# One loop per engine for two attention branches, with branch A's sums folded behind the loops

## The chip, the cores and the metric

The kernel runs on one core of a Trainium2 chip. The metric is the device time of one execution in microseconds. The engines are named as the profile names them: PE multiplies matrices (PEld is its loading of weights), DVE works on vectors, ACT on scalars and activations, POOL is GpSimd, and SP issues the loads.

## What is computed

Two attention branches, A and B, decode one token for two batch entries from a cache of 4096 tokens, 32 heads of 128 elements, all in float32. A gate mixes them. Cut to what matters:

```python
def branch(x, k_cache, v_cache, wq, wo):      # x: 2 x 1 x 512, caches: 2 x 32 x 4096 x 128
    q = heads_of(x @ wq)                      # wq: 512 x 4096
    p = softmax(q @ k_cache^T * 128 ** -0.5)  # over the 4096 tokens
    return rows_of(p @ v_cache) @ wo          # wo: 4096 x 512

g = sigmoid((A_x * gate_w).sum(-1))
out = g * branch(A_x, A_...) + (1 - g) * branch(A_x, B_...)
```

The work is hardly more than reading four caches of 134 MB each once.

## The kernel before

**Tiling.** A unit of work is one branch, one group `g` of four heads (`NG = 8` groups) and one batch entry `b`. There are `NU = 32` units, all of A's before all of B's. A unit's K block and V block are 8 MB each: 128 partitions, on each of them 128 tokens of 128 elements, 32 partitions to a head. K blocks alternate between the two tiles `kt`, V blocks share one tile `vt`. `wq` of both branches comes through `kt` before the first units, and `wo` of both after the last ones (A's into the tile that holds even units, B's into the other).

**The loads.** SP issues all large loads in one written order (lines 516 to 526): `wq` of A, the first K block, `wq` of B, then K and V by turns, `wo` of A, the last V block in three parts, `wo` of B in six parts. In front of a K load it waits until DVE has read the tile's last block (`k_free`), in front of a V load until PE has (`v_free`).

**A unit.** DVE multiplies the K block by the query (line 391) and sums it to scores (394). It takes the maxima over a head (399 to 401) and spreads the next query (404, 405). ACT makes the exponentials (365) into `padded` and their sums into a column of `lp`. PE multiplies them by V in 64 matmuls (`products`, line 369) and adds up both batch entries of a group in the PSUM tile `vp`. When a group is through, ACT (452) and DVE (415) add `vp` into `vs[:, g]`.

**The end of a branch.** `sum_of` (lines 467 to 470) makes the denominators from `lp`, times the gate. `gather` (473) collects `vs[:, g]` in the PSUM tile `heads`, two matmul records for each of the eight groups. `deal_out` scales them on ACT (478), puts them in the order that `wo` wants with 16 matmul records against the table `deal` (482), and copies the result to `on[n]` (485). `project_out` (497) multiplies by `wo`. The last rows of B's `wo` are done in four strips (512), and the rest, `most`, is folded into them (609, 612) with `fold`, which is made from an identity that POOL writes (589, 590, 592).

**Loops.** The engines run free of each other and meet at semaphores. PE, DVE and ACT have hardware loops of their own. Each branch has its own loops over its first seven groups: DVE and ACT leave theirs for the last group of A. In that straight part DVE does A's `sum_of`, PE A's eight gathers and `deal` matmuls, and ACT A's copies (`branch_sums`, and the argument `between` of `dve_first` and `act_first`); then the loops of B begin. PE's first loop takes 16 units, its second 15. A's projection stands behind PE's second loop, and B's last unit and end follow it. The table `deal` is built by DVE in the first microseconds (313 to 318), from the identity that lies in `vt` then.

All of this is written out by hand inside one unscheduled part (`tile_critical`, line 179).

Of the kernel before, what the change touches and what calls it, by code (L numbers as in the profile page):

```python
# [7 lines left out]
F32 = mybir.dt.float32  # L8
# [5 lines left out]
B = 2  # L14
# [6 lines left out]
NG = H // G  # L21
NS = SK // PH
# [119 lines left out]
def tile_gated_decode(ctx: ExitStack, tc: tile.TileContext, ins: dict, out: bass.AP):  # L142
# [9 lines left out]
    gate = {n: small.tile([P, 1], F32, name="gate" + n) for n in "AB"}  # L152
# [15 lines left out]
    nil = small.tile([P, 1], F32, name="nil")  # L168
# [10 lines left out]
    with tc.tile_critical():  # L179
# [10 lines left out]
        r_vs = [R() for _ in range(NG)]  # L190
# [122 lines left out]
        put("dve", lambda x: x.memset(deal, 0.0), [], [r_deal])  # L313
        for b in range(B):
            for k in range(DQ):
                piece = R()
                piece.writers = r_deal.writers[:1]
                vput("dve", lambda x: x.tensor_copy(deal[:, b, k, :, :, k], ident.rearrange(
                    "p (h g b) -> p b g h", h=G, b=B)[:, b, :NG]), [r_ident], [piece])
        r_deal.writers = piece.writers  # L320
# [4 lines left out]
        def project(n):  # L325
            i_k = place["wq", n]
            if n == "A":
                room, mark = Scratch(vt, 8 * P + D), lambda p: r_vt.readers.append(p)
            else:
                room, mark = Scratch(kt[i_k]), lambda p: None  # L330
            halves = kt[i_k].rearrange("p r d -> p (r d)").rearrange(
                "p (c i g h d) -> p c i h g d", c=KC, i=NG // STRIPS, h=G, d=DH)
            for i, t in enumerate(qa):
                put("dve", lambda x: x.memset(t, 0.0), [], [r_qa[i]])
            for c in range(KC):
                arrived("pe", ("wq", n), *((c * len(parts["wq", n]) // KC,)))
                for i, t in enumerate(qa):
                    for h in range(G):
                        put("pe", lambda x: x.matmul(t[h * QT:h * QT + B], cols[:, c], halves[:, c, i, h],  # L339
                                                     start=c == 0, stop=c == KC - 1), [r_cols, *r_kt[i_k]], [r_qa[i]])  # L340
# [10 lines left out]
            mark(put("dve", lambda x: x.tensor_copy(qcol[n], wide.rearrange("p (g k b) -> p g k b", g=NG, b=QT)[:, :, :, :B]),  # L351
                     [r_wide], [r_qcol[n]]))
            for r in r_kt[i_k]:
                r.readers += r_wide.readers

        def spread_queries(u):
            n, g, b = units[u]
            put("dve", lambda x: x.tensor_copy(qsel, qcol[n][:, g:g + 1, :, b:b + 1]), [r_qcol[n]], [r_qsel])
            put("dve", lambda x: x.transpose(q, qsel[:, 0].to_broadcast([P, DH // QT, QT])), [r_qsel], [r_q])
# [43 lines left out]
        def next_queries(n, g, b):  # L403
            at = D_.do(lambda x: x.tensor_copy(qsel, qcol[n][:, g, :, b:b + 1]))  # L404
            return D_.do(lambda x: x.transpose(q, qsel[:, 0].to_broadcast([P, DH // QT, QT])), at)  # L405

        def dve_second(nxt):
            take("dve", k_landed[1], 16)
            maxima_of(1, whole_scores(1, 0))
            return next_queries(*nxt, 0) if nxt else 0  # L410
# [7 lines left out]
        def dve_first(g, nxt, at, between=None):  # L418
# [4 lines left out]
            if between:  # L423
                between()
            maxima_of(0, at)
            next_queries(*nxt, 1)
# [27 lines left out]
        def act_first(g, col, between=None):  # L454
# [5 lines left out]
            if between:  # L460
                between()
# [3 lines left out]

        def sum_of(n):
            put("dve", lambda x: x.transpose(across, lp), [r_lp], [r_across])
            put("dve", lambda x: x.tensor_reduce(rs, across, axis=AX.X, op=ALU.add), [r_across], [r_rs])
            put("dve", lambda x: x.reciprocal(rs, rs), [], [r_rs])
            put("dve", lambda x: x.tensor_tensor(rs, rs, gate[n], op=ALU.mult), [r_gate[n]], [r_rs])  # L470

        def gather(g):
            put("pe", lambda x: x.matmul(heads, pick[:, (NG - g) * B:][:, :P], vs[:, g], start=g == 0, stop=g == NG - 1),
                [r_pick, r_vs[g]], [r_heads])

        def deal_out(n):
            t = vs[:, 0]
            put("act", lambda x: x.activation(t, heads, AF.Copy, scale=rs), [r_heads, r_rs], [r_vs[0]])
            dealt = bank[:, :B * OR].rearrange("p (b r) -> p b r", b=B)
            for b in range(B):  # L480
                for k in range(DQ):
                    put("pe", lambda x: x.matmul(dealt[:, b], deal[:, b, k].rearrange("p g h q -> p (g h q)"),
                                                 t[:, k * OR:(k + 1) * OR], start=k == 0, stop=k == DQ - 1),
                        [r_deal, r_vs[0]], [r_bank])
# [59 lines left out]
        def step(e, n, lo, hi, second, first):  # L544
            with nc.Fori(lo, hi, engines=[{"dve": mybir.EngineType.DVE, "act": mybir.EngineType.Activation}[e]]) as i:
                first(i, second(i))

        def dve_pairs(n):
            S.wait("dve", [*r_q.writers, (S.sems["dve"], S.ticks["dve"])])
            with nc.Fori(0, NG - 1, engines=[mybir.EngineType.DVE]) as i:  # L550
                nxt = n, bass.ds(i + 1, 1)
                at = dve_second(nxt)
                dve_first(i, nxt, at)

        def act_pairs():
            with nc.Fori(0, NG - 1, engines=[mybir.EngineType.Activation]) as i:
                act_second(bass.ds(i * B + 1, 1))
                act_first(i, bass.ds(i * B + B, 1))
# [23 lines left out]
        end = Scratch(kt[place["wo", "A"]]).take  # L582
        ident2, fold, onb, kept = end(P), end(QT), end(OR * B), end(D)
        totals = [end(D // OS)[:B].rearrange("b (s e) -> b s e", s=STRIPS // OS) for _ in range(OS)]
        on["B"] = onb.rearrange("p (r b) -> p r b", b=B)
        r_ident2, r_fold, r_kept, r_total = R(), R(), R(), [R(), R()]
        for r in (r_ident2, r_fold, r_kept, r_on["B"], *r_total):
            r.readers = [p for x in r_kt[place["wo", "A"]] for p in x.readers]
        put("pool", lambda x: x.memset(ident2, 0.0), [], [r_ident2])
        put("pool", lambda x: x.affine_select(out=ident2, in_=ident2, compare_op=ALU.not_equal, fill=1.0, base=0,  # L590
                                              pattern=[[-1, P]], channel_multiplier=1), [], [r_ident2])
        put("dve", lambda x: x.tensor_reduce(fold, ident2.rearrange("p (s q) -> p q s", s=STRIPS), axis=AX.X, op=ALU.add),  # L592
            [r_ident2], [r_fold])
        sum_of("B")
        for g in range(NG - 1):
            r_vs[g].writers = r_rs.writers
            gather(g)
        last_products()
        take_out(NG - 1)
        take("dve", taken)  # L600
        for a in range(1, VC):
            put("dve", lambda x: x.scalar_tensor_tensor(  # L602
                vs[:, NG - 1], vp[:, a * DH:(a + 1) * DH], slot[:, a:a + 1], vs[:, NG - 1], op0=ALU.mult, op1=ALU.add),
                [r_vs[NG - 1]] if a > 1 else [], [r_vs[NG - 1]] if a > 1 else [])
            r_vs[NG - 1].writers = [(S.sems["dve"], S.ticks["dve"])]
        gather(NG - 1)
        deal_out("B")
        project_out("B", EARLY)
        put("act", lambda x: x.activation(kept, most, AF.Copy), [r_most], [r_kept])  # L609
# [6 lines left out]
        for i, e in enumerate(("dve", "act")):  # L616
            for j in range(STRIPS // OS):
                k = (i * STRIPS // OS + j) * QT
                src = acc[i][k:k + B, :D // STRIPS]
                put(e, (lambda x: x.activation(totals[i][:, j], src, AF.Copy)) if i else  # L620
                    (lambda x: x.tensor_copy(totals[i][:, j], src)), [r_qa[i]], [r_total[i]])  # L621
            landed.append(S.dma("act" if i else "sp", out.rearrange("b o (i s e) -> (b o) i s e", i=OS, s=STRIPS // OS)[:, i],
                                totals[i], reads=[r_total[i]], slot="x"))
# [23 lines left out]
```

## Time and profile before

| | before |
|---|---|
| median of 3 runs | 1324.59 us (1324.45 to 1324.62) |
| the profiled execution | 1324.58 us |
| its span, first to last instruction | 1322.8 us |
| read from memory | 570.43 MB, 431 GB/s over the span |
| busy: DVE, PE, ACT | 1166.3, 343.3, 101.4 us |
| mean granted clock of PE | 0.627 of full speed |

A row of the timeline begins with its start and its duration in microseconds; then come the engine, the line of the kernel, the operation, what it writes and reads, and how many records the row merges. In brackets stands how long the engine had been idle and what ended that. A "q" behind an engine's name is its instruction queue. A row of the table by stretches gives the stretch, its length, the busy time and number of instructions of PE, PEld, DVE, ACT and POOL, then PE's granted clock, the share of DMA engines that were busy and GB/s. Matmuls overlap, so a merged row's duration is that of the whole stretch and the mean of one record is longer than the spacing.

### The profile page before, as it was taken

The numbers are of one execution on the slowest core, as the hardware profiler recorded it, in microseconds if no ns is written. First come the engines' busy times: TensorE is split into PE (matmuls) and PEld (weight loads), VectorE is DVE, ScalarE is ACT, GpSimd is POOL, SyncE is SP. The second block draws the span as 40 slices with busy tenths as digits, with TensorE's granted clock in tenths as the row PEclk, the third lists the DMA queues.
The fourth block names the chain that finished last, engine by engine and source line by source line (L and its number), as shares of the span: only waits on it lengthen the run. The fifth ranks groups of instructions, "written<-read, shape, count | busy, mean of one in ns | idle before, by whom it ended". The sixth has DMA issues, their size and how long they took to land. (4 is left out here: it accounts for less than half of the span.)

```text
span 1322.8 us, 6257 instructions
## 1 busy us (share of the span) xinstructions
PE 343.3 (26%) x2406; PEld 100.7 (8%) x2406; DVE 1166.3 (88%) x321; ACT 101.4 (8%) x331; POOL 1.2 (0%) x8
## 2 busy tenths in 40 slices
PE   3202222202222221222224022222212222221256
PEld 0000000000000000000002000000000000000012
DVE  2399999999999999999999899999999999999960
ACT  0000000001010000101000010100001010000100
POOL 0000000000000000000000000000000000000000
PEclk9656666556666655666665566666566666656668
DMA  9999999999999999999999999999999999999998
GB/s 412 442 414 442 442 416 442 444 414 444 442 430 428 442 442 416 442 442 416 444 442 419 438 442 434 426 440 440 420 440 440 420 442 442 426 432 442 434 420 357
DMA packets 11109, 570.53 MB, mean 431 GB/s; under 512 B 1239, under 2 KB 1243, under 8 KB 1630
## 3 DMA queue, kind: packets, MB, share of 16 engines
q1 hardware_dynamic: 11092, 570.43, 99.6%
q8 instruction: 4, 0.07, 0.0%
q14 instruction: 3, 0.02, 0.0%
q10 hardware_dynamic: 10, 0.01, 0.0%
HBM read 570.43 MB, written 0.00 MB: 431 GB/s over the span
## 5 line engine op out<-in xcount | busy, mean ns | idle before, releaser
L391 DVE TENSOR_TENSOR kt<-kt,q 128x16384 f32<-128x16384 f32 x31 | 534.0, 17226 | 56.1 <-DVEq L95 56.0
L394 DVE TENSOR_REDUCE sc<-kt 128x128 f32<-128x16384 f32 x31 | 533.8, 17220 | 1.1
L369 PE MATMUL vp<-vt,pr 128*32 128x512 f32 x2048 | 291.8, 733 | 919.3 <-PEq L95 918.5
L369 PEld LDWEIGHTS vp<-vt,pr 128*32 128x32 f32 x2048 | 80.3, 132 | 1129.3 <-issue 1126.9
L365 ACT ACTIVATE pr<-sc,nm 32x128 f32<-32x128 f32 x128 | 50.9, 398 | 160.0 <-ACTq L95 118.2
L431 ACT ACTIVATE pr<-nil 128x512 f32<-128x512 f32 x31 | 19.3, 624 | 426.4 <-ACTq L95 426.4
L452 ACT ACTIVATE vs<-vp,slot 128x128 f32 (+1 forms) x16 | 5.9, 368 | 451.6 <-ACTq L95 451.6
L339 PE MATMUL qa<-kt,cols 128*2 128x512 f32 x128 | 18.7, 741 | 22.9 <-DMA kt<-in_B_wq_dram 15.7
L365 ACT ACTIVATION_READ_ACCUMULATOR pr<-sc,nm (+1 forms) x128 | 23.5, 184 | 0.0
L350 DVE STREAM_TRANSPOSE kt<-kt 128x1024 f32<-128x1024 f32 x1 | 1.2, 1246 | 23.5 <-ACT kt L348 23.5
L415 DVE SCALAR_TENSOR_TENSOR vs<-vp,slot,vs 128x128 f32 (+1 forms) x45 | 15.8, 351 | 6.3 <-DVEq L95 5.3
L534 DVE TENSOR_REDUCE sc<-kt 128x64 f32<-128x8192 f32 x2 | 17.4, 8686 | 0.1
L533 DVE TENSOR_TENSOR kt<-kt,q 128x8192 f32<-128x8192 f32 x2 | 17.4, 8686 | 0.0
L459 ACT ACTIVATE vp<-nil 128x512 f32<-128x512 f32 x15 | 9.0, 600 | 106.6 <-ACTq L95 106.6
L621 DVE COPY kt<-qa 2x128 f32<-2x128 f32 x2 | 0.6, 280 | 17.0 <-PE qa L512 17.0
L592 DVE TENSOR_REDUCE kt<-kt 128x32 f32<-128x128 f32 x1 | 0.4, 368 | 12.8 <-POOL kt L590 12.8
L497 PE MATMUL most<-kt,onA 128*2 128x512 f32 x64 | 8.6, 698 | 9.5 <-DMA kt<-in_A_wo_dram 9.5
L399 DVE TENSOR_REDUCE rm<-sc 128x1 f32<-128x128 f32 x31 | 8.7, 282 | 2.3
L405 DVE STREAM_TRANSPOSE q<-qsel 128x128 f32<-128x128 f32 x30 | 9.3, 311 | 1.3 <-DVE qsel L404 0.3
L602 DVE SCALAR_TENSOR_TENSOR vs<-vp,slot,vs 128x128 f32<-128x128 f32 x3 | 1.1, 352 | 10.6 <-DVEq L95 10.6
L350 DVE STREAM_TRANSPOSE vt<-vt 128x1024 f32<-128x1024 f32 x1 | 1.2, 1246 | 9.4 <-ACT vt L348 9.4
L497 PE MATMUL most<-kt,kt 128*2 128x512 f32 x56 | 8.6, 779 | 2.4 <-DMA kt<-in_B_wo_dram 2.4
(68 smaller groups left out, 72.9 us busy)
## 6 DMA issues: line engine op xcount, KB each, us to landing
kt<-in_A_wq_dram SPq DMA_DIRECT2D x2, 4096.0 KB, 16.6
kt<-in_A_k_cache_dram SPq DMA_DIRECT2D x2, 4096.0 KB, 29.0
vt<-in_B_v_cache_dram SPq DMA_DIRECT2D x1, 4096.0 KB, 18.3
kt<-in_B_wo_dram SPq DMA_DIRECT2D x1, 4096.0 KB, 33.1
vt<-in_B_v_cache_dram SPq DMA_DIRECT2D x1, 3072.0 KB, 25.2
kt<-in_B_wo_dram SPq DMA_DIRECT2D x1, 2048.0 KB, 37.5
vt<-in_B_v_cache_dram SPq DMA_DIRECT2D x1, 1024.0 KB, 27.2
kt<-in_B_wo_dram SPq DMA_DIRECT2D x1, 1024.0 KB, 39.5
```

What stands on the lines that cost most here:

```text
L339: put("pe", lambda x: x.matmul(t[h * QT:h * QT + B], cols[:, c], halves[:, c, i, h], start=c == 0, stop=c == KC - 1), [r_cols, *r_kt[i_k]] ...
L365: do(lambda x: x.activation(padded[h, :, b, j * VC:(j + 1) * VC], s[h].rearrange("p (c a) -> p c a", a=VC), AF.Exp, bias=m[h], accum_out=l ...
L369: return x.matmul(vp[c % STRIPS * QT:(c % STRIPS + 1) * QT], padded[:, c].rearrange("p b m -> p (b m)"), vt[:, c * VC:(c + 1) * VC].rearra ...
L391: at = D_.do(lambda x: x.tensor_tensor(kt[o], kt[o], q[:, None, :].to_broadcast([P, NS, DH]), op=ALU.mult), after)
L394: at = D_.do(lambda x: x.tensor_reduce(sc[o], kt[o], axis=AX.X, op=ALU.add), at)
L405: return D_.do(lambda x: x.transpose(q, qsel[:, 0].to_broadcast([P, DH // QT, QT])), at)
L415: at = D_.do(lambda x: x.scalar_tensor_tensor(vs[:, g], vp[:, a * DH:(a + 1) * DH], slot[:, a:a + 1], vs[:, g], op0=ALU.mult, op1=ALU.add) ...
L431: return A_.do(lambda x: x.activation(padded[:, :, b], nil[:, :, None].to_broadcast([P, NVC, G * VC]), AF.Copy))
L459: A_.do(lambda x: x.activation(vp, nil.to_broadcast([P, VC * DH]), AF.Copy))
L497: put("pe", lambda x: x.matmul(most[s * QT:s * QT + B], on[n][:, r], wo[n][:, r], start=n == "A" and r < STRIPS, stop=n == "B" and r >= EA ...
L533: put("dve", lambda x: x.tensor_tensor(t, t, q[:, None, :].to_broadcast([P, NS // 2, DH]), op=ALU.mult), [r_q], [r])
L534: put("dve", lambda x: x.tensor_reduce(sc[0][:, h * NS // 2:(h + 1) * NS // 2], t, axis=AX.X, op=ALU.add), [r], [R()])
```

## The change

1. The loops of both branches become one for each engine: PE's takes 31 units, DVE's and ACT's 15 of the 16 groups of both branches (`NA = 16`). `vs` has 16 groups, `qcol` holds both branches' queries, and `lp` has 32 columns for the units and 16 more that stay at one.
2. A's end moves behind the loops. DVE makes both sums there. PE's order is then: A's gathers, A's `deal` matmuls, B's gathers but the last, A's projection, the last unit's products, B's last gather, B's `deal` matmuls, B's projection.
3. `deal` is no tile of its own. It is built behind the loops in the A half of `vs`, once A's gathers have read that. The identity comes to lie in `q`, the fold and B's `on` in `sc[1]`, the scaled heads in `sc[0]`, `kept` and the totals in the B half of `vs`.
4. The unscheduled part ends without a drain of GpSimd.

The diff, cut to its core:

```diff
-    lp = small.tile([P, PH], F32, name="lp")
+    lp = small.tile([P, PH + PH // 2], F32, name="lp")
...
-    deal = small.tile([P, B, DQ, NG, G, DQ], F32, name="deal")
-    qcol = {n: small.tile([P, NG, DH // QT, B], F32, name="qcol" + n) for n in "AB"}
+    qcol = small.tile([P, NA, DH // QT, B], F32, name="qcol")
...
-    vs = small.tile([P, NG, DH], F32, name="vs")
+    vs = small.tile([P, NA, DH], F32, name="vs")
...
-    with tc.tile_critical():
+    with tc.tile_critical(no_gpsimd_drain=True):
...
-        put("dve", lambda x: x.memset(deal, 0.0), [], [r_deal])
-        for b in range(B):
-            for k in range(DQ):
-                piece = R()
-                piece.writers = r_deal.writers[:1]
-                vput("dve", lambda x: x.tensor_copy(deal[:, b, k, :, :, k], ident.rearrange(
-                    "p (h g b) -> p b g h", h=G, b=B)[:, b, :NG]), [r_ident], [piece])
-        r_deal.writers = piece.writers
...
+        def build_deal():
+            put("dve", lambda x: x.memset(vs[:, :NG], 0.0), [], [r_deal, *r_vs[:NG]])
+            pieces = []
+            for b in range(B):
+                for k in range(DQ):
+                    pieces.append(R())
+                    pieces[-1].writers = r_deal.writers
+                    put("dve", lambda x: x.tensor_copy(deal[:, b, k, :, :, k], ident2.rearrange(
+                        "p (h g b) -> p b g h", h=G, b=B)[:, b, :NG]), [r_ident2], [pieces[-1]])
+            r_deal.writers = pieces[-1].writers
...
-        products(NU // 2)
-        dve_pairs("A")
-        act_pairs()
-        at = dve_second(("B", slice(0, 1)))
-        act_second(slice(PH // 2 - 1, PH // 2))
-
-        def branch_sums():
-            sum_of("A")
-            for g in range(NG):
-                r_vs[g].writers = r_rs.writers
-                gather(g)
-
-        dve_first(NG - 1, ("B", slice(0, 1)), at, branch_sums)
-        act_first(NG - 1, slice(0, 1), lambda: deal_out("A"))
-        products(NU // 2 - 1)
-        project_out("A", OR)
-        dve_pairs("B")
-        act_pairs()
+        products(NU - 1)
+        S.wait("dve", [*r_q.writers, (S.sems["dve"], S.ticks["dve"])])
+        with nc.Fori(0, NA - 1, engines=[mybir.EngineType.DVE]) as i:
+            nxt = bass.ds(i + 1, 1)
+            at = dve_second(nxt)
+            dve_first(i, nxt, at)
+        with nc.Fori(0, NA - 1, engines=[mybir.EngineType.Activation]) as i:
+            act_second(bass.ds(i * B + 1, 1))
+            act_first(i, bass.ds(i * B + B, 1))
         dve_second(None)
-        act_second(slice(PH // 2 - 1, PH // 2), last=True)
+        act_second(slice(NU - 1, NU), last=True)
         D_.close()
...
-        sum_of("B")
-        for g in range(NG - 1):
-            r_vs[g].writers = r_rs.writers
-            gather(g)
+        for n in "AB":
+            sum_of(n)
+        for r in (r_ident2, *r_vs[:-1]):
+            r.writers = r_rs.writers
...
+        for j in range(NG):
+            gather(j)
+        build_deal()
+        deal_out("A")
+        for j in range(NG, NA - 1):
+            gather(j)
+        project_out("A", OR)
         last_products()
-        take_out(NG - 1)
+        take_out(NA - 1)
```

More of the change, by code (lines that the diff above doesn't have):

```diff
@@ L151, in tile_gated_decode @@
     cols = small.tile([P, KC, B], F32, name="cols")
-    gate = {n: small.tile([P, 1], F32, name="gate" + n) for n in "AB"}
+    few = small.tile([P, 8], F32, name="few")
+    gate, nil = {n: few[:, i:i + 1] for i, n in enumerate("AB")}, few[:, 2:3]
     padded = small.tile([P, NVC, B, G * VC], F32, name="pr")
-    lp = small.tile([P, PH], F32, name="lp")
+    lp = small.tile([P, PH + PH // 2], F32, name="lp")
     slot = small.tile([P, VC], F32, name="slot")
     pick = small.tile([P, NG * B + P], F32, name="pick")
-    deal = small.tile([P, B, DQ, NG, G, DQ], F32, name="deal")
-    qcol = {n: small.tile([P, NG, DH // QT, B], F32, name="qcol" + n) for n in "AB"}
+    qcol = small.tile([P, NA, DH // QT, B], F32, name="qcol")
     qsel = small.tile([P, 1, DH // QT, 1], F32, name="qsel")
@@ L189, in tile_gated_decode @@
         r_qa = [R(), R()]
-        r_vs = [R() for _ in range(NG)]
+        r_vs = [R() for _ in range(NA)]
         sem = tc.alloc_semaphore
@@ L350, in project @@
             mark(put("dve", lambda x: x.transpose(wide, qrow), r_qrow, [r_wide]))
-            mark(put("dve", lambda x: x.tensor_copy(qcol[n], wide.rearrange("p (g k b) -> p g k b", g=NG, b=QT)[:, :, :, :B]),
+            mark(put("dve", lambda x: x.tensor_copy(qcol[:, "AB".index(n) * NG:][:, :NG], wide.rearrange("p (g k b) -> p g k b", g=NG, b=QT)[:, :, :, :B]),
                      [r_wide], [r_qcol[n]]))
@@ L356, in spread_queries @@
         def spread_queries(u):
[L357 to L358 removed]
+            j, b = divmod(u, B)
+            put("dve", lambda x: x.tensor_copy(qsel, qcol[:, j:j + 1, :, b:b + 1]), [r_qcol[units[u][0]]], [r_qsel])
             put("dve", lambda x: x.transpose(q, qsel[:, 0].to_broadcast([P, DH // QT, QT])), [r_qsel], [r_q])
@@ L409, in dve_second @@
             maxima_of(1, whole_scores(1, 0))
-            return next_queries(*nxt, 0) if nxt else 0
+            return next_queries(nxt, 0) if nxt is not None else 0
         def add_out(g, last):
@@ L416, in add_out, with dve_first @@
                                                             op0=ALU.mult, op1=ALU.add), at, last if a == VC - 1 else None)
-        def dve_first(g, nxt, at, between=None):
+        def dve_first(g, nxt, at):
             take("dve", k_landed[0], 16)
@@ L422, in dve_first @@
             add_out(g, added)
-            if between:
-                between()
             maxima_of(0, at)
-            next_queries(*nxt, 1)
+            next_queries(nxt, 1)
             D_.close()
@@ L452, in take_out, with act_first @@
             A_.do(lambda x: x.activation(vs[:, g], vp[:, :DH], AF.Copy, scale=slot[:, :1]), 0, taken)
-        def act_first(g, col, between=None):
+        def act_first(g, col):
             take_out(g)
@@ L472, in gather @@
-        def gather(g):
-            put("pe", lambda x: x.matmul(heads, pick[:, (NG - g) * B:][:, :P], vs[:, g], start=g == 0, stop=g == NG - 1),
-                [r_pick, r_vs[g]], [r_heads])
+        deal = vs.rearrange("p g d -> p (g d)")[:, :NG * DH].rearrange(
+            "p (b k g h q) -> p b k g h q", b=B, k=DQ, g=NG, h=G)
+        ident2 = q
+        kept = vs.rearrange("p g d -> p (g d)")[:, NG * DH:][:, :D]
+        totals = [vs.rearrange("p g d -> p (g d)")[:, NG * DH + D:][:, i * D // OS:(i + 1) * D // OS][:B].rearrange(
+            "b (s e) -> b s e", s=STRIPS // OS) for i in range(OS)]
@@ new lines, in tile_gated_decode @@
+        sums = {"A": rm, "B": rs}
+        r_sums = {"A": r_rm, "B": r_rs}
+        on["B"] = sc[1][:, :OR * B].rearrange("p (r b) -> p r b", b=B)
+        fold = sc[1][:, OR * B:][:, :QT]
+        r_ident2, r_fold, r_kept, r_total, r_dealt = R(), R(), R(), [[R(), R()], [R(), R()]], R()
+        def sum_of(n):
+            t, r = sums[n], r_sums[n]
+            put("dve", lambda x: x.transpose(across, lp[:, "AB".index(n) * PH // 2:][:, :PH]), [r_lp], [r_across])
+            put("dve", lambda x: x.tensor_reduce(t, across, axis=AX.X, op=ALU.add), [r_across], [r])
+            put("dve", lambda x: x.reciprocal(t, t), [], [r])
+            put("dve", lambda x: x.tensor_tensor(t, t, gate[n], op=ALU.mult), [r_gate[n]], [r])
@@ new lines, in gather @@
+        def gather(j):
+            g = j % NG
+            put("pe", lambda x: x.matmul(heads, pick[:, (NG - g) * B:][:, :P], vs[:, j], start=g == 0, stop=g == NG - 1),
+                [r_pick, r_vs[j]], [r_heads])
+        def build_deal():
[8 more added lines that the diff above has]
+            r_deal.writers = pieces[-1].writers
@@ L476, in deal_out @@
         def deal_out(n):
-            t = vs[:, 0]
-            put("act", lambda x: x.activation(t, heads, AF.Copy, scale=rs), [r_heads, r_rs], [r_vs[0]])
+            t = sc[0]
+            put("act", lambda x: x.activation(t, heads, AF.Copy, scale=sums[n]), [r_heads, r_sums[n]], [r_sc])
             dealt = bank[:, :B * OR].rearrange("p (b r) -> p b r", b=B)
@@ L542, in tile_gated_decode @@
         exps(0, 0, slice(0, 1), lambda make, gives: put("act", make, [r_nm[0], r_sc, r_pad, r_lp, r_nil], [], gives))
[L544 to L553, printed above, removed]
@@ L585, in tile_gated_decode @@
[L585 to L588, printed above, removed]
+        r_sc.writers = r_sc.readers = []
+        for n in "AB":
+            sum_of(n)
+        for r in (r_ident2, *r_vs[:-1]):
+            r.writers = r_rs.writers
         put("pool", lambda x: x.memset(ident2, 0.0), [], [r_ident2])
@@ L602, in tile_gated_decode @@
             put("dve", lambda x: x.scalar_tensor_tensor(
[L603 to L606, printed above, removed]
+                vs[:, NA - 1], vp[:, a * DH:(a + 1) * DH], slot[:, a:a + 1], vs[:, NA - 1], op0=ALU.mult, op1=ALU.add),
+                [r_vs[NA - 1]] if a > 1 else [], [r_vs[NA - 1]] if a > 1 else [])
+            r_vs[NA - 1].writers = [(S.sems["dve"], S.ticks["dve"])]
+        gather(NA - 1)
         deal_out("B")
         project_out("B", EARLY)
+        r_kept.readers = [p for r in r_vs[NG:-1] for p in r.readers]
         put("act", lambda x: x.activation(kept, most, AF.Copy), [r_most], [r_kept])
```

27 lines of the change are left out of this document (8 added, 19 removed).

## The prediction

> **What bounds the kernel now.** I read the head of the page first, then the chain of work that ended last.
>
> ```profile
> span 1322.8 us, 6257 instructions
> PE 343.3 (26%) x2406; PEld 100.7 (8%) x2406; DVE 1166.3 (88%) x321; ACT 101.4 (8%) x331; POOL 1.2 (0%) x8
> DMA  9999999999999999999999999999999999999998
> ```
>
> ```profile
> 1258.91 17.23 DVE sc L394
> 1276.21 33.05 DMA kt<-in_B_wo_dram
> 1309.31 8.70 PE most L497 x56
> 1318.03 0.61 ACT kt L609
> ```
>
> The DMA row holds 9 in every slice but the last: the load stream is never empty. DVE at 88% comes second. The chain says the same of the end: it follows the loads of `wo` of B, and only the last ten microseconds belong to PE, ACT and the store of the output. Next the loop, from the timeline of DVE.
>
> ```profile
> 661.81 17.23 DVE L391 TENSOR_TENSOR kt<-kt,q 128x16384 f32<-128x16384 f32 x1 [2.88 <-DVEq L95]
> 700.40 17.23 DVE L391 TENSOR_TENSOR kt<-kt,q 128x16384 f32<-128x16384 f32 x1 [0.91 <-DVEq L95]
> 739.46 17.23 DVE L391 TENSOR_TENSOR kt<-kt,q 128x16384 f32<-128x16384 f32 x1 [3.21 <-DVEq L95]
> 778.06 17.23 DVE L391 TENSOR_TENSOR kt<-kt,q 128x16384 f32<-128x16384 f32 x1 [1.53 <-DVEq L95]
> ```
>
> In front of each multiplication DVE sits waiting (the wait of line 95, for a K block to land). It waits 0.91 us even at 700.40, where today's hand-over from A to B adds four small operations to DVE. So the hand-over hides behind the loads, and taking it out of the loop frees time on engines that have time. One thing may be won there: the spacings are 38.59, 39.06 and 38.60 us, and the middle one, right after the hand-over, is longer by some 0.46. If the hand-over makes that, it goes.
>
> **What is taken away at the start.** The table `deal` is no longer built there.
>
> ```profile
> 13.64 0.91 DVE L313 MEMSET deal<- 128x1024 f32 x1 [0.16 <-issue]
> 14.59 0.88 DVE L318 COPY deal<-vt 128x32 f32<-128x32 f32 x8
> 42.08 9.87 PE L339 MATMUL qa<-kt,cols 128*2 128x512 f32 x64 [15.74 <-DMA kt<-in_B_wq_dram]
> ```
>
> From 13.64 to 15.47 that is 1.83 us of DVE, ahead of A's query projection. But PE then waits 15.74 us for `wq` of B, which the load stream brings when it can. I take the gain as nothing; the wait for that load covers it eight times over. The merged tiles (`few`, `qcol`, the longer `vs` and `lp`), the single loops of 15 rounds and the indices over 16 groups change no operation's size; I cost them at nothing, under the 0.91 us or more that DVE waits for each K block, and they would cost once that cover were gone.
>
> **What lands at the end.** A's sums, its eight gathers (16 matmuls), the building of `deal`, A's `deal` matmuls and the projection of A now stand one behind another ahead of the last products in PE's order. Their prices come from the hand-over of today, and those of the rest from today's end.
>
> ```profile
> 698.46 3.78 PE L473 MATMUL heads<-vs,pick 128*128 128x128 f32 x16 [7.84 <-DVE rs L470]
> 702.70 3.62 PE L482 MATMUL bank<-vs,deal 128*128 128x32 f32 x16 [0.46 <-ACT vs L478]
> ```
>
> ```profile
> 1279.00 0.18 ACT L365 ACTIVATION_READ_ACCUMULATOR pr<-sc,nm 32x1 f32 x1
> 1280.23 8.61 PE L497 MATMUL most<-kt,onA 128*2 128x512 f32 x64 [9.51 <-DMA kt<-in_A_wo_dram]
> ...
> 1290.07 0.20 DVE L467 STREAM_TRANSPOSE across<-lp 128x32 f32<-128x32 f32 x1
> ...
> 1290.72 0.16 DVE L470 TENSOR_TENSOR rs<-rs,gateB 128x1 f32<-128x1 f32 x1
> 1290.93 1.83 PE L473 MATMUL heads<-vs,pick 128*128 128x128 f32 x14 [2.09 <-DVE rs L470]
> ...
> 1297.15 3.64 PE L369 MATMUL vp<-vt,pr 128*32 128x512 f32 x32 [0.81 <-DMA vt<-in_B_v_cache_dram]
> ...
> 1300.94 0.37 ACT L452 ACTIVATE vs<-vp,slot 128x128 f32<-128x128 f32 x1 [21.76 <-ACTq L95]
> ...
> 1303.16 0.37 ACT L478 ACTIVATE vs<-heads,rs 128x128 f32<-128x128 f32 x1 [1.85 <-PE heads L473]
> ...
> 1303.58 3.35 PE L482 MATMUL bank<-vs,deal 128*128 128x32 f32 x16 [0.46 <-ACT vs L478]
> ...
> 1306.96 0.22 ACT L485 ACTIVATE kt<-bank 128x64 f32<-128x64 f32 x1 [3.44 <-PE bank L482]
> 1309.31 8.57 PE L497 MATMUL most<-kt,kt 128*2 128x512 f32 x56 [2.38 <-DMA kt<-in_B_wo_dram]
> ```
>
> The same kind of work has two prices: 16 gathers took 3.78 us in the middle and 14 took 1.83 at the end. The table by stretches shows why; the last three numbers of a row are the granted clock, the DMA share and GB/s, and the first pair is PE's busy time with its matmuls.
>
> ```profile
> 699.80:703.10 3.30, 2.84 (x14) 2.55 (x14) 2.70 (x1) 0.37 (x1) 0.00 (x0) 0.50 0.78 338
> 703.20:706.40 3.20, 3.13 (x15) 2.99 (x15) 3.20 (x1) 0.04 (x1) 0.00 (x0) 0.50 1.35 579
> ...
> 1280.20:1283.40 3.20, 3.17 (x16) 0.55 (x20) 0.00 (x0) 0.00 (x0) 0.00 (x0) 0.50 1.04 451
> 1283.50:1288.80 5.30, 5.30 (x52) 1.05 (x44) 0.00 (x0) 0.00 (x0) 0.00 (x0) 1.00 0.97 414
> ...
> 1293.70:1303.80 10.10, 6.98 (x64) 1.97 (x55) 1.05 (x3) 0.74 (x2) 0.00 (x0) 1.00 1.03 440
> 1304.00:1307.00 3.00, 2.92 (x14) 2.79 (x14) 0.00 (x0) 0.04 (x1) 0.00 (x0) 0.50 0.91 393
> 1309.30:1314.10 4.80, 4.79 (x24) 0.85 (x28) 0.00 (x0) 0.00 (x0) 0.00 (x0) 0.50 0.96 406
> 1314.20:1318.00 3.80, 3.79 (x41) 0.78 (x36) 0.00 (x0) 0.00 (x0) 0.00 (x0) 1.00 0.85 340
> ```
>
> The wide matmuls of the projection run at clock 0.50 for 3.2 us and then at 1.00 (16 in 3.17 us, 0.20 each; then 52 in 5.30, 0.10 each). The gathers and the `deal` matmuls kept PE busy for over 7 us around 700 and the clock stayed at 0.50. So I price the added gathers and `deal` matmuls at half clock. The Trainium skill, "TensorE: Matmul & The Clock Gate", section "What's actually happening", says that about 3.4 us of sustained activity bring the full clock; the rows at 699.80 and 703.20 do not agree for this kind of matmul. By that rule the end would come out as the first rival below.
>
> Now the path, on the clock of this trace. `lp` is whole at 1279.18. One sum takes from 1290.07 to 1290.88, so two take 1.62; with the hand-offs PE starts A's gathers at 1281.0 (its other input, all of `vs` but the last, is long there). They end after 3.78, at 1284.8. Beside ACT's copy (0.37) DVE builds `deal` in its new place, the A half of `vs`, which it may overwrite only once the gathers have read it: 1.83 and the hand-offs, 1286.7. A's `deal` matmuls, 3.62: 1290.3. B's seven gathers, 14 matmuls at 3.78/16: 3.3, 1293.6; beside them ACT writes `onA`. The projection of A, 8.61 as today from half clock: 1302.2. The last products, all landed by then, 64 matmuls at 3.64 per 32: 7.3, 1309.5. Today they end at 1300.79. A second way to the same 8.7: added are 3.78, 1.9 of waiting, 3.62, 1.5 for gathers that are slow instead of fast, and a start 0.8 later, 11.6 in all; PE's waits of 2.09 and 0.81 us take up 2.9.
>
> From there on it is today's chain. ACT starts 0.15 after the products, at 1309.65; 2.64 later come B's `deal` matmuls. They take 3.35 at mostly half clock, 1.8 at the full one (half of 3.62). The clock fell about 3 us after the last product today, so they get some of each: 2.3. With ACT's copy `onB` is ready at 1314.85 instead of 1307.18. Now the 2.38 us that PE waited for `wo` at 1309.31 take up a part, and all but the last loads have landed: 56 matmuls, between 5.6 (all full clock) and some 9 (half clock for up to 6 us); today 8.57, with short waits in it; I take 7.9 and get 1322.75 instead of 1317.88. What follows (L609 and the last rows) hangs on that end as it does today. Sum: plus 4.9.
>
> **What comes off.** The 0.46 in the middle: between nothing and 0.46, I take 0.4, since the end hangs on the last K block. The drain of GpSimd:
>
> ```profile
> 1320.27 0.26 ACTq L104 DMA_DIRECT2D out_dram<-kt  x1
> ...
> L179 POOLq DRAIN  x1: 41/41/41, 1321.7 to 1321.7; - x1
> ```
>
> Line 179's drain stands at 1321.7 and lasts 41 ns, with an exchange of semaphores around it. Its bounds are nothing and 2.3 us (from the end of the issue at 1320.53 to the end of the span); the drain's own row is the near one, and I take 0.3 with the exchange. GpSimd's other work, the identity and the strip fold from it, is needed only by the last matmuls and sits beside the gathers.
>
> Sum against the profiled execution: 1324.58 (its span and 1.78 around it; the median of the runs is 1324.59) plus 4.9, minus 0.4, minus 0.3: 1328.8.
>
> **The rivals.**
> *The clock rises on the gathers: no change.* Then only the first 3.4 us are slow: gathers 3.78, waiting 1.9, `deal` 1.8, gathers 1.83, projection 6.4 (64 at 0.10), products 7.0, so 1303.7 instead of 1309.5; `onB` comes near 1308.6, under the 1309.31 at which `wo` lands. The end is the load stream's again and the time 1324.58 − 0.7 = 1323.9. For it: the gathers at 1290.93 ran fast, though behind wide matmuls. Against it: the two rows at 700. It decides from `onB` before 1309.31. Chance 0.10.
> *The end outside the loads shrinks: faster.* If the drain's exchange is worth all of its upper bound and the PE chain hides as in the first rival, it is 1324.58 − 0.4 − 2.3 = 1321.9. For it: 2.3 us do lie between the issue of the output and the end of the span. Against it: the store has to land within them, and the drain's own row is 41 ns. It passes the bound only with a drain over 2.3 us. Chance 0.04.
> *A worse phase of the clock: slower still.* B's `deal` at 3.35 and the 56 matmuls at 9.4 (half clock for twice 3.4 us) move the end to 1325.3 and the time to some 1331.3; a longer stay at half clock, or a code load in PE's now longer straight part, goes past 1332. Chance of past 1332: 0.06. The Trainium skill, same page and section, calls the clock's window free-running, so that the change comes at another matmul from run to run; the rows here show only one execution.
>
> **How the numbers follow.** Forecast 0.80, rivals 0.10, 0.04 and 0.06. The forecast's own spread comes from the clock: with `deal` of B at 1.8, 7.0 for the 56 matmuls and a projection of A that is fast all through (6.4 for 8.61), the sum falls by 0.5, 0.9 and 2.2 to 1325.2; the other end is 1331.3. The range is 1325.2 to 1332.0. A measurement of this kernel can tell about 0.2%, 2.65 us, from no change, so same reaches up to 1327.2: the first rival and 0.05 of the forecast, 0.15. Slower gets the other 0.75 of the forecast and the third rival, 0.81; faster 0.04.
>
> **What would show it.** Right: DVE's spacing of L391 stays at 38.6 all through, A's gathers start near 1281 at clock 0.50 and last near 3.8; PE has no wait for a V part or for `wo` of B behind them; the matmuls of B's projection start near 1315 with ACT's `onB` as releaser instead of a DMA; the chain of work that ended last runs over PE from about 1281 on. Wrong: a releaser `in_B_wo` at the start of B's projection (the chain hides), a clock of 1.00 over A's `deal` matmuls, or an end of the load stream that has moved itself.

## The result and the profile after

The changed kernel takes 1328.55 us (median of 8 runs, 1327.94 to 1328.93), the kernel before 1324.61 us in the same comparison (8 runs, 1324.45 to 1324.94). The ratio is 1.0029, with a 95% interval of 1.002 to 1.0038: slower by 3.9 us. The prediction was 1328.8 us.

The profiled execution of the changed kernel took 1327.94 us, with a span of 1326.2, so against the profiled one of before it is 3.36 us longer. It is the fastest of the eight, so the rows below show the best case. The head of its page and the chain that ended last:

```profile
span 1326.2 us, 6272 instructions
DMA  9999999999999999999999999999999999999997
...
PE 1%; ACT 0%; DVE 0%; issue 0%
PE most L510 1%; PE bank L495 0%; DVE vs L592 0%; ACT vs L600 0%; PE qa L525 0%; ACT vs L612 0%; PE heads L475 0%; PE qa L603 0%; ACT sc L491 0%; ACT sc L498 0%
```

The load stream is as full as before up to the last slice, but the loads of `wo` are gone from the chain: it is PE with short pieces of DVE and ACT. The view follows the chain back only to 1307.49, where DVE takes over the last products; further back it has to be read from PE's rows. PE's rows of the timeline behind its loop (numbers of the new lines: 475 gathers, 495 `deal` matmuls, 510 projections, 361 products):

```profile
1280.35 3.79 PE L475 MATMUL heads<-vs,pick 128*128 128x128 f32 x16 [10.26 <-DVE rs L471]
1286.30 3.62 PE L495 MATMUL bank<-sc,vs 128*128 128x32 f32 x16 [2.16 <-DVE vs L485]
1289.73 3.32 PE L475 MATMUL heads<-vs,pick 128*128 128x128 f32 x14
1292.98 7.05 PE L510 MATMUL most<-kt,onA 128*2 128x512 f32 x64
1299.84 7.05 PE L361 MATMUL vp<-vt,pr 128*32 128x512 f32 x64
1308.74 0.49 PE L475 MATMUL heads<-vs,pick 128*128 128x128 f32 x2 [1.85 <-DVE vs L592]
1309.69 3.40 PE L495 MATMUL bank<-sc,vs 128*128 128x32 f32 x16 [0.46 <-ACT sc L491]
1313.49 7.81 PE L510 MATMUL most<-kt,sc 128*2 128x512 f32 x56 [0.40 <-ACT sc L498]
```

From 1280.35 on PE never waits for a load. It waits 2.16 us for DVE to finish `deal` (line 485), and at 1313.49 the projection of B waits for ACT, where before it waited 2.38 us for `wo`. The last products end at 1306.89 instead of 1300.79. ACT's rows that wait for them and for the matmuls behind them, and the issue of the output:

```profile
1307.05 0.37 ACT L442 ACTIVATE vs<-vp,slot 128x128 f32<-128x128 f32 x1 [16.88 <-ACTq L96]
...
1313.12 0.22 ACT L498 ACTIVATE sc<-bank 128x64 f32<-128x64 f32 x1 [3.49 <-PE bank L495]
1321.45 0.60 ACT L600 ACTIVATE vs<-most 128x512 f32<-128x512 f32 x1 [8.10 <-PE most L510]
...
1323.67 0.26 ACTq L105 DMA_DIRECT2D out_dram<-vs  x1
```

The copy of `most` starts at 1321.45 instead of 1318.03 (3.42 later), the output is issued at 1323.67 instead of 1320.27 (3.40 later), and from there it is 2.53 us to the end of the span in both kernels. DVE's large multiplications around the old hand-over, and the granted clock along PE's new chain (the third number from the end of a row):

```profile
700.24 17.23 DVE L383 TENSOR_TENSOR kt<-kt,q 128x16384 f32<-128x16384 f32 x1 [1.53 <-DVEq L96]
738.92 17.23 DVE L383 TENSOR_TENSOR kt<-kt,q 128x16384 f32<-128x16384 f32 x1 [2.83 <-DVEq L96]
777.52 17.23 DVE L383 TENSOR_TENSOR kt<-kt,q 128x16384 f32<-128x16384 f32 x1 [1.53 <-DVEq L96]
```

```profile
1286.10:1289.40 3.30, 3.10 (x15) 3.11 (x15) 0.14 (x2) 0.00 (x0) 0.00 (x0) 0.50 0.96 412
1289.60:1292.80 3.20, 3.20 (x16) 3.17 (x15) 0.00 (x0) 0.22 (x1) 0.00 (x0) 0.50 0.97 415
1293.00:1300.00 7.00, 7.00 (x69) 1.81 (x72) 0.00 (x0) 0.00 (x0) 0.00 (x0) 1.00 1.06 453
...
1310.00:1313.30 3.30, 3.08 (x15) 2.95 (x14) 0.00 (x0) 0.18 (x1) 0.00 (x0) 0.50 0.95 405
1313.50:1316.70 3.20, 3.20 (x16) 0.55 (x20) 0.00 (x0) 0.00 (x0) 0.00 (x0) 0.50 0.99 404
```

The spacing that was 39.06 us is 38.68 now. The clock was at 0.50 for the gathers and the `deal` matmuls, as priced, but went to 1.00 at 1292.8, within the last of B's gathers, so the whole projection of A had it.

### The profile page after: what moved, and what is told of

Read it like the earlier page. It is cut to its first block, busy times and chain, and to the rows that moved or that the text cites. A ratio compares the mean times of both kernels' runs of the same rounds, so it can differ in the third digit from the quotient of the medians.

```text
span 1326.2 us, 6272 instructions
## 1 busy us (share of the span) xinstructions
PE 343.3 (26%) x2406; PEld 102.5 (8%) x2406; DVE 1166.4 (88%) x321; ACT 101.4 (8%) x331; POOL 1.2 (0%) x8
## 5 line engine op out<-in xcount | busy, mean ns | idle before, releaser
L421 ACT ACTIVATE pr<-few 128x512 f32<-128x512 f32 x31 | 19.3, 623 | 436.7 <-ACTq L96 436.7
L407 DVE SCALAR_TENSOR_TENSOR vs<-vp,slot,vs 128x128 f32 x45 | 15.8, 351 | 6.5 <-DVEq L96 5.4
L449 ACT ACTIVATE vp<-few 128x512 f32<-128x512 f32 x15 | 9.0, 600 | 105.7 <-ACTq L96 105.7
L475 PE MATMUL heads<-vs,pick 128*128 128x128 f32 x32 | 7.6, 424 | 12.1 <-DVE rs L471 10.3
L475 PEld LDWEIGHTS heads<-vs,pick 128*128 128x128 f32 x32 | 6.9, 323 | 13.9 <-DVE rs L471 11.2
L510 PE MATMUL most<-kt,sc 128*2 128x512 f32 x56 | 7.8, 717 | 0.4 <-ACT sc L498 0.4
```

Source lines behind the costliest of these rows:

```text
L407: at = D_.do(lambda x: x.scalar_tensor_tensor(vs[:, g], vp[:, a * DH:(a + 1) * DH], slot[:, a:a + 1], vs[:, g], op0=ALU.mult, op1=ALU.add) ...
L421: return A_.do(lambda x: x.activation(padded[:, :, b], nil[:, :, None].to_broadcast([P, NVC, G * VC]), AF.Copy))
L510: put("pe", lambda x: x.matmul(most[s * QT:s * QT + B], on[n][:, r], wo[n][:, r], start=n == "A" and r < STRIPS, stop=n == "B" and r >= EA ...
```

## The experiments

The theory: the loss is PE's longer order behind the loops, at half clock for its small matmuls; merged loops and the missing drain cost and bring nothing. The rivals: the end moved for another cause (the loads, the drain), the added work lies beside other work, or the gathers are dear for another reason than the clock.

**The flag alone,** on the kernel before:

```diff
-    with tc.tile_critical():
+    with tc.tile_critical(no_gpsimd_drain=True):
```

> The kernel before, with GpSimd's drain at the end left out and nothing else changed. Theory of the PE chain (all of the loss is PE's longer order behind the loops, the flag is worth next to nothing): 1324.6 us, within 0.1 of the kernel before, and 2.53 us from the issue of the output on ACT to the end of the span, as before. Rival (the flag is worth the 0.3 us that the prediction took, or up to 2.3): 1324.3 down to 1322.3.

Measured 1324.63 us against 1324.69, ratio 1.0 (0.9991 to 1.0009). The rows of GpSimd's queue at line 179 and of the output's issue in this run:

```profile
1320.16 0.26 ACTq L104 DMA_DIRECT2D out_dram<-kt  x1
...
L179 POOLq NOP  x1: 13/13/13, 1321.6 to 1321.6; - x1
```

A NOP of 13 ns stands where the drain of 41 ns stood, and it comes 1.4 us behind the issue in both. The interval of the ratio, 1.2 us to either side, would leave room for the prediction's 0.3 us, but the trace does not show them: from the issue to the end of the span it is 2.53 us in the kernel before, 2.44 here and 2.53 again in the changed kernel, which has the flag too. So the flag is worth nothing that can be measured here.

**A's gathers first.** They move in front of the sums, right behind PE's loop:

```diff
         products(NU - 1)
+        for j in range(NG):
+            gather(j)
...
-        for r in (r_ident2, *r_vs[:-1]):
+        for r in (r_ident2, *r_vs[NG:-1]):
             r.writers = r_rs.writers
...
-        for j in range(NG):
-            gather(j)
         build_deal()
```

> The changed kernel, but A's eight gathers stand right behind PE's loop and no longer wait for the sums (they do not need them). PE is idle there from 1270 to 1280. Theory of the PE chain: A's deal matmuls then wait for the building of deal alone, which can start after the strip fold at 1281.4 and ends at 1283.3, so they start near 1283.4 instead of 1286.3, and all behind moves by 2.9 us: about 1325.6 us, with a spread of 0.7 from the clock's phase. Rival (the end waits for something else, such as the loads of wo): no change from 1328.5.

Measured 1325.81 us (1325.06 to 1328.44), ratio 1.001 (1.0 to 1.0019). PE's rows:

```profile
1269.34 2.05 PE L475 MATMUL heads<-vs,pick 128*128 128x128 f32 x16
1283.51 3.62 PE L495 MATMUL bank<-sc,vs 128*128 128x32 f32 x16 [12.12 <-DVE vs L485]
...
1310.66 8.48 PE L510 MATMUL most<-kt,sc 128*2 128x512 f32 x56 [0.41 <-ACT sc L498]
```

The `deal` matmuls start at 1283.51 (1283.4 was expected), 2.8 us earlier than in the changed kernel, and the projection of B starts 2.8 us earlier. The median is 2.7 us lower. What is taken off in front of PE's chain comes off at the end. (In the profiled executions B's projection took 8.48 us instead of 7.81, so 2.15 of the 2.8 us are left at the copy of `most`, 1319.30 instead of 1321.45.)

**The gathers and `deal` first.** On top of that, the identity and `deal` are made ahead of the sums, with a small DVE operation behind the last scores to let GpSimd begin (shown against the changed kernel, without the lines of the gathers, which move as above):

```diff
-        for n in "AB":
-            sum_of(n)
-        for r in (r_ident2, *r_vs[:-1]):
-            r.writers = r_rs.writers
+        put("dve", lambda x: x.memset(few[:, 3:4], 0.0), [], [r_ident2])
         put("pool", lambda x: x.memset(ident2, 0.0), [], [r_ident2])
...
+        build_deal()
+        for n in "AB":
+            sum_of(n)
+        for r in r_vs[NG:-1]:
+            r.writers = r_rs.writers
...
-        build_deal()
         deal_out("A")
```

> As the run with A's gathers first, and the identity and deal are also built ahead of the sums, while ACT makes the last exponentials. Theory of the PE chain: A's deal matmuls start when ACT has scaled the heads, near 1280.1 instead of 1286.3, 6.2 us earlier; the last products end near 1302.0, B's result is ready near 1308.5, and PE waits for wo of B again (it lands at 1309.1): the end is the load stream's, 1324.0 to 1324.3 us, which is 0.3 to 0.6 under the kernel before if the 0.46 us in the middle stay away. Rival (PE's order is not the cause): 1327 or more.

Measured 1325.11 us (1324.46 to 1326.15), ratio 1.0002 (0.9993 to 1.0011).

```profile
1280.31 3.59 PE L495 MATMUL bank<-sc,vs 128*128 128x32 f32 x16 [8.74 <-DVE rs L470]
...
1309.46 6.74 PE L510 MATMUL most<-kt,sc 128*2 128x512 f32 x48 [2.43 <-DMA kt<-in_B_wo_dram]
```

The releaser of B's projection is the load again, after 2.43 us of waiting. So with merged loops and A's sums behind them the kernel is back at the time of before, within the interval; PE's order, with its waits, is what cost. The median is still 0.4 us above the kernel before, but not in the span: its median is 1322.9 us in both. The time around the span is what differs. It was 1.7 to 1.9 us in every run of the kernel before whose span is on record, but up to 3.1 here and up to 2.4 in the changed kernel; nothing here shows what it is. The further gain of 0.3 to 0.6 us that I expected is not there: `wo` lets PE start at 1309.46, before it was 1309.31. What was saved in the middle is no longer there when the loads end; why is not shown.

**The building of `deal` left out** of the changed kernel:

```diff
-        build_deal()
+        r_deal.writers = r_rs.writers
```

> The changed kernel without the building of deal (its matmuls read the A half of vs as it stands, so the result is meaningless). Theory of the PE chain: A's deal matmuls start when ACT has scaled the heads, near 1284.6 instead of 1286.3, and all behind moves by 1.7 us: 1326.8 us, with 0.7 to either side from the clock's phase. Rival (the building lies beside other work): 1328.5.

Measured 1326.05 us (1324.37 to 1328.74), ratio 1.0013 (1.0003 to 1.0023); the profiled execution is the 1324.37.

```profile
1284.57 1.97 PE L495 MATMUL bank<-sc,vs 128*128 128x32 f32 x16 [0.46 <-ACT sc L491]
...
1309.19 6.74 PE L510 MATMUL most<-kt,sc 128*2 128x512 f32 x48 [0.83 <-DMA kt<-in_B_wo_dram]
```

The start is the expected 1284.6, and the median is 2.5 us lower, a little more than the 1.7 and up to 0.7 more that were expected. In the profiled execution, the fastest of the ten, the same 16 matmuls took 1.97 us instead of 3.62, at full clock, and so the whole chain hid. The runs lie 4.4 us apart (their spans 3.1), where I had allowed 0.7 to either side.

**The clock raised,** with 72 added records on PE while it waits for the sums:

```diff
         products(NU - 1)
+        for _ in range(36):
+            put("pe", lambda x: x.matmul(acc[0][:B], pick[:, :B], vs[:, :4].rearrange("p g d -> p (g d)"), start=True, stop=True),
+                [r_pick], [r_qa[0]])
```

> The changed kernel with 36 added wide matmuls (72 records) of old data into a PSUM tile that is free then, between PE's loop and A's gathers, where PE is idle anyway; they add work that nothing uses. Theory (the gathers are dear because the granted clock is 0.50 there): clock 1.00 at A's gathers, which take 2.1 us instead of 3.79, and part of the gain goes on to the deal matmuls and B's gathers: 1.5 to 4 us less, 1324.5 to 1327.0 us. Rival (the gathers are dear for another reason, such as their loads of weights): 3.8 us as before at clock 1.00, and 1328.5 us.

Measured 1346.12 us: the added matmuls were mis-sized. They all went to one strip of the array and lasted past 1300.

```profile
1270.25 31.06 PE L559 MATMUL qa<-vs,pick 128*2 128x512 f32 x72
1301.24 2.05 PE L475 MATMUL heads<-vs,pick 128*128 128x128 f32 x16
1305.45 1.97 PE L495 MATMUL bank<-sc,vs 128*128 128x32 f32 x16 [2.15 <-DVE vs L485]
```

The time says nothing, but the rows behind them do: gathers 2.05 us instead of 3.79, `deal` matmuls 1.97 instead of 3.62. The repetition deals the same 72 records over the four strips (`s = i % STRIPS * QT`, output `acc[0][s:s + B]`):

> As the run that was to raise the clock, with the added 72 records dealt over all four strips of the PE array, as the projection's are, so that they take about 9 us (16 at 0.20, the rest at 0.10) and end before 1280. Theory (half clock makes the gathers and deal matmuls dear): clock 1.00 there, 2.05 us instead of 3.79 for A's gathers and about 2 instead of 3.62 for its deal matmuls, as in the run before; B's gathers may fall back to 3.3. The chain moves by 1.7 to 3.4 us: 1325.2 to 1326.8 us. Rival (the clock is not the price): 1328.5.

Measured 1325.88 us (1324.71 to 1328.09), ratio 1.0011 (1.0001 to 1.0021).

```profile
1270.38 7.91 PE L560 MATMUL qa<-vs,pick 128*2 128x512 f32 x72
1280.80 2.05 PE L475 MATMUL heads<-vs,pick 128*128 128x128 f32 x16 [2.51 <-DVE rs L471]
1285.01 2.23 PE L495 MATMUL bank<-sc,vs 128*128 128x32 f32 x16 [2.15 <-DVE vs L485]
```

Work that nothing uses makes the changed kernel 2.7 us faster, within the 1.7 to 3.4 expected. Half clock is the price of these matmuls: shown.

**What raises the clock.** The rows around 700 of the kernel before had led me to say that neither kind of matmul does. Two runs take one kind each, by doing A's `deal` matmuls or A's gathers three times over.

```diff
-            for b in range(B):
+            for b in [b for _ in range(3 if n == "A" else 1) for b in range(B)]:
```

> The changed kernel with A's deal matmuls done three times over (the same result), 48 records instead of 16. Theory (this kind of matmul, 32 columns for each load of 128 weights, does not raise the granted clock however long it lasts): clock 0.50 all along, 10.9 us instead of 3.62, the time near 1335.8. Rival (any matmul that fills a window raises the clock): full clock after 3.4 to 6.8 us, the 48 records in 7.0 to 8.7 us, the time near 1332.5.

```diff
-        for j in range(NG):
+        for j in 3 * [*range(NG)]:
             gather(j)
```

> The changed kernel with A's eight gathers done three times over (the same result), 48 records instead of 16. Theory (a window of the clock that gathers fill from end to end raises it, other than one filled by deal matmuls): between 14 and 29 records at half clock (0.236 each), the rest at the full one (0.128), 7.7 to 9.4 us in all, and the deal matmuls behind them partly fast. Rival (the prediction's: gathers do not raise the clock): 0.50 all along and 11.3 us.

Measured 1334.52 us (1335.8 was expected) and 1331.44 us, one run each. PE's rows and the clock, `deal` first:

```profile
1286.45 10.45 PE L495 MATMUL bank<-sc,vs 128*128 128x32 f32 x48 [2.15 <-DVE vs L485]
...
1286.50:1296.80 10.30, 10.30 (x49) 10.30 (x49) 0.00 (x0) 0.00 (x0) 0.00 (x0) 0.50 0.97 417
...
1296.72 3.33 PE L475 MATMUL heads<-vs,pick 128*128 128x128 f32 x14
1299.98 8.25 PE L510 MATMUL most<-kt,onA 128*2 128x512 f32 x64
```

Now the gathers:

```profile
1280.88 8.28 PE L475 MATMUL heads<-vs,pick 128*128 128x128 f32 x48 [10.32 <-DVE rs L471]
...
1280.60:1284.00 3.40, 3.12 (x14) 3.13 (x15) 0.56 (x3) 0.00 (x0) 0.50 (x2) 0.50 1.05 453
1284.20:1291.00 6.80, 4.96 (x35) 4.77 (x33) 1.52 (x8) 0.37 (x1) 0.00 (x0) 0.83 1.02 437
```

The `deal` matmuls (32 columns for each load of weights) kept PE busy for 10.45 us and the clock stayed at 0.50. The gathers (128 columns) took 8.28 us instead of 11.3, and the clock rose within them, some 5.5 us after the first. (The second stretch's 0.83 is a mean: 0.50 up to 1286.3, 1.00 from 1286.8 on.) The prediction weighed the rule of the Trainium skill ("TensorE: Matmul & The Clock Gate", section "What's actually happening") that about 3.4 us of sustained activity bring the full clock. In these runs that does not hold for the `deal` matmuls, and for the gathers the clock rises, but later. Whether 16 gathers, 3.8 us, are enough differs between executions of the same code. In the kernel before the clock was still at 0.50 behind those of the middle; in the run with the flag alone, which has the same code there, the `deal` matmuls right behind them ran at full clock:

```profile
698.90:702.30 3.40, 3.25 (x16) 2.96 (x14) 2.44 (x4) 0.11 (x1) 0.00 (x0) 0.50 0.80 347
702.50:705.70 3.20, 1.97 (x16) 1.86 (x16) 3.20 (x1) 1.11 (x6) 0.00 (x0) 1.00 1.11 476
```

B's 14 gathers are the same: in the changed kernel the clock was at 1.00 right behind them, in the run with `deal` three times the clock's mean over the next 3 us was 0.59, and the projection took 8.25 us instead of 7.05. That the phase of the clock against the work decides fits all these rows, but no run varied that phase alone.

**PE's loop in two,** for the 0.38 us in the middle:

```diff
-        products(NU - 1)
+        products(NU // 2)
+        products(NU // 2 - 1)
```

> The changed kernel with PE's single loop cut in two loops of 16 and 15 units; nothing of the hand-over's work comes back. Theory (the 0.46 us in the middle belong to the load of 16 KB of code for PE's second loop, which shares the load stream): one spacing of DVE's large multiplications near 700 is 39.0 instead of 38.6, the last K block lands near 1241.5 instead of 1241.0, PE's chain starts 0.4 later, and the time is 0.4 more, 1328.9 within 0.7. Rival (the hand-over's gathers, sums and copies made it): all spacings 38.6 and 1328.5.

Measured 1326.55 us in one run.

```profile
700.34 17.23 DVE L383 TENSOR_TENSOR kt<-kt,q 128x16384 f32<-128x16384 f32 x1 [1.53 <-DVEq L96]
739.14 17.23 DVE L383 TENSOR_TENSOR kt<-kt,q 128x16384 f32<-128x16384 f32 x1 [2.95 <-DVEq L96]
777.75 17.23 DVE L383 TENSOR_TENSOR kt<-kt,q 128x16384 f32<-128x16384 f32 x1 [1.54 <-DVEq L96]
```

The spacing is 38.80. It is 38.68 or 38.69 in all nine traces with one loop, and 39.06 and 39.04 in the two with the loops of before. So PE's second loop accounts for 0.12 us, less than the 0.4 expected, and where the other 0.26 come from stays open. That the 0.12 are a load of code is not shown; what fits is the profile's queue for instructions, which has four packets here and in the kernel before (0.07 MB) and three in the changed kernel (0.05 MB). The time missed its expectation by 1.7 us beyond the allowed spread. This one execution had A's `deal` matmuls at 2.48 us; it does not bear on the question.

**All of it,** gathers and `deal` first, and 76 added records (over four strips) between A's gathers and its `deal` matmuls:

```diff
         for j in range(NG):
             gather(j)
+        for i in range(38):
+            s = i % STRIPS * QT
+            put("pe", lambda x: x.matmul(acc[0][s:s + B], pick[:, :B], vs[:, NG:NG + 4].rearrange("p g d -> p (g d)"), start=True, stop=True),
+                [r_pick], [r_qa[0]])
```

> The kernel with A's gathers and deal first, and with 38 added wide matmuls (76 records that nothing uses) on PE between A's gathers and its deal matmuls, where PE waits for the sums. Theory of the PE chain: the clock is at 1.00 more of the time up to A's projection, the chain hides behind the loads of wo in every phase of the clock, and the time is that of the loads, 1324.2 to 1324.7 us with a spread as small as the kernel before has; no less, since the loads end where they ended before. Rival (a gain is still to be had from the hand-over's 0.36 us in the middle): 1324.0 to 1324.2.

Measured 1324.62 us (1324.19 to 1325.33) against 1324.67, ratio 0.9999 (0.999 to 1.0008).

```profile
1281.05 1.97 PE L495 MATMUL bank<-sc,vs 128*128 128x32 f32 x16
...
1309.55 8.34 PE L510 MATMUL most<-kt,sc 128*2 128x512 f32 x56 [2.02 <-DMA kt<-in_B_wo_dram]
```

PE has 2.02 us to spare at the load of `wo`, and the time is that of the kernel before. The runs lie 1.1 us apart, instead of 1.7 without the added work; but the spans lie 1.1 apart instead of 0.7, so the added work did not bring the spans closer: what is smaller is the time around the span, 1.7 to 1.8 us in every run here. None of these versions beats it: where PE's chain hides, the load stream sets the end, and that has not moved.

## Why the prediction was right

The main step held: A's end landed in front of the last products in PE's order, and what the slack did not take up came out at the end. Step by step, predicted and measured in the profiled execution:

| | predicted | measured |
|---|---|---|
| A's gathers start | 1281.0 | 1280.35 |
| A's `deal` matmuls start | 1286.7 | 1286.30 |
| A's projection lasts | 8.61 | 7.05 |
| last products end | 1309.5 | 1306.89 |
| B's `deal` matmuls last | 2.3 | 3.40 |
| B's result on ACT (`onB`) is ready | 1314.85 | 1313.34 |
| B's projection lasts | 7.9 | 7.81 |
| off at the end for the drain | 0.3 | 0 |

- The start came 0.65 earlier, 0.48 of it because DVE's last scores begin earlier (1258.43 instead of 1258.91), most of which is the middle's excess that is gone, as taken (0.4 for 0.38). The 0.46 that the prediction read was too much: around the middle the spacings of both kernels alternate between 38.6 and 38.7, and it compared with the shorter ones. The gain counts while PE's chain sets the end. In the three profiled executions in which the chain hid, `wo` let B's projection start at 1309.46, 1309.55 and 1309.19, against 1309.31 and, with the flag alone, 1309.21: it is not in the end of the loads.
- The largest term that was mis-sized is A's projection, 1.56 us too long. The step behind it is the sentence that the gathers leave the clock at half, from which the projection was to start: here the clock rose within B's gathers, right ahead of the projection. It need not have: in the run with `deal` three times the projection took 8.25 us. B's `deal` matmuls were 1.1 us too short, by the same uncertainty about where the clock falls.
- The start at the front was priced at nothing, and so was the merging; the last run, in which A's end hides and the time is that of before, bears both out, to within its interval (1.2 us to either side).
- The drain's 0.3 us was an allowance for an exchange of semaphores that stays: only the drain itself became a NOP.
- That the median came within 0.25 us of the forecast is partly luck. The terms missed by 0.3 to 1.6 us, in both directions; the profiled execution is 0.86 us under the forecast, and the median is 0.61 above that execution.
- The first rival, a chain that hides at full clock, was a real alternative. A hidden chain was there in the profiled execution of the run without the building of `deal`, and in those of the two runs with the gathers and `deal` first. A clock of 1.00 over A's gathers and `deal` matmuls was not enough: in the run with the clock raised, B's `deal` matmuls took 3.52 us, and B's projection, at 1310.81, still waited for ACT. In the changed kernel as it stands, none of 8 runs came near it.

The clock's phase was expected to spread the forecast from 1325.2 to 1331.3. The changed kernel's runs lie within 1.0 us, those of its variants up to 4.4 us apart (spans within 1.1 and up to 3.4). Why some spread more than others was not tried, and only the profiled executions show what the clock did.

## What to carry to other kernels

Here the work beside the full load stream cost nothing that was left at the end of the loads, and taking it out of there gained nothing. Moved between the last K block and the last products, on the engine that makes the end, each microsecond of it counts once the slack there is used up. Before moving work to the end, list what the engine that does it waits for there (here 2.09, 0.81 and 2.38 us) and price the work at the clock that it may find, half or full. If it must go to the end, start what depends on nothing late first: the gathers needed no sums, and that order alone gave back 2.7 of the 3.9 us.

## What the runs showed of the hardware

- Matmuls with 32 columns for each load of 128 weights left the granted clock at 0.50 through 10.45 us of unbroken work; matmuls with 128 columns raised it, some 5.5 us after the first of 48, and in some executions not within the 3.8 us of 16.
- At the same full clock, 72 records of two-column weights and 512 columns took 31.06 us on one strip of the array and 7.91 us over four, 0.43 and 0.11 us each.
- Adding useless matmuls in an idle stretch made the changed kernel faster by 2.7 us: the clock behind them was at 1.00, and the 16 gathers took 2.05 us instead of 3.79.
